# A fused attention and gated-FFN kernel: when its tail asks for its loads and forms its weight sums

## The chip, the cores and the metric

The kernel runs on one core of one Trainium2 chip. The metric is the device time of one execution in microseconds (us); the time before is the median of three runs.

Engines are named as in the profile: PE is TensorE (PEld its weight loads), DVE is VectorE, ACT is ScalarE, POOL is GpSimd, and SP is the engine whose queue issues most DMA transfers here.

## The reference

For `x` of 2048 rows and 512 columns, two branches are computed and mixed with a gate per row:

```python
g = _sigmoid((x * gate_w).sum(-1, keepdims=True))
a = _A_ref(x, A_wqkv, A_wo)              # attention, 32 heads of 16, causal window of 256, then @ wo
b = (_silu(x @ w_gate) * (x @ w_up)) @ w_down     # w_gate, w_up: 512 x 1792, w_down: 1792 x 512
return g * a + (1 - g) * b
```

## The kernel before, in words

Everything is kept transposed: features lie on the 128 partitions, positions along the rows, in four chunks `c` of 512 positions. An f32 product is made of three matmuls (`mm3`, L88 to L90): each operand is split into a rounded high part and a low part, and high x high, high x low and low x high are added up in PSUM. The split of an operand (`split`) costs one ACT instruction for the high part (L70) and one DVE instruction for the low part (L73).

The body computes attention, and beside it the gate and up products of the FFN. Attention's heads go to a DRAM tile `od`, the FFN's activated products to a DRAM tile `kept_h` (14 row tiles `f`, 4 chunks). The **tail** (class `B` in the code, from L685 on) does what is left:

1. `last_tile(c)` for the four chunks: the last FFN tile (L770, 24 matmuls each). Between them the weights `wo` are split (`late`).
2. Sixteen items `("a", c, k)`: the output projection of attention. An item has 12 matmuls. After the fourth item of a chunk four PSUM banks hold its result; DVE multiplies each with the gate (`attn`, L905 or L902) and POOL's queue sends it to `outT`. Even chunks use the banks `ps1` and `ps2`, odd ones `pa` and `pb`, so item 8 writes banks that items 0 to 3 filled.
3. The down projection by a Strassen-Winograd scheme: seven products in the order `ORDER = (1, 5, 6, 3, 7, 2, 4)`, 14 items of 6 matmuls each. The item with index `WO` = 16 is the first of product 1.

The operands of the seven products are made of four quarters of `kept_h`, called `x`, `v`, `y` and `z` (L814), 14 pieces `j` of 256 KB each: product 1 takes x, 5 takes v, 6 takes v + z, 3 takes z, 7 takes (v + z) - x, 2 takes y and 4 takes v + z + y. `combine` (L817) makes the sums on DVE. On the weights' side product 1 takes the left half of `w_down` (`load_left`, L753, then a split), and products 5, 6, 3 and 7 take sums of blocks: `sums(k)` for k = 4, 5, 6 loads two tiles of `w_down` (L185), forms four block sums on DVE (L192, four instructions), splits them (`high` on ACT, L846; `low` on DVE, L850) and stores them in a DRAM tile `sd` (L854), from where `load_sum` (L837) brings them back into the tiles `wh` and `wl`, about 6 items ahead of use.

The order in every queue is the order of the code. The main loop goes over the items `n`; in each round it issues a load of an attention item (`got<-od`, L738), then what the table `DO[n]` holds (filled with `on(n, ...)` and `steps`), then `load_sum`, then the split of item n + LEAD (`halve`, LEAD = 4), then one job (`JOBS`: the evacuation of a PSUM bank), and then the item's matmuls:

```python
for n, e in enumerate(ITEMS[:end]):
    if n + LEAD + AHEAD < WO: load(ITEMS[n + LEAD + AHEAD])
    for f in DO.pop(n, ()): f()
    ...
    if n + LEAD < len(ITEMS): halve(ITEMS[n + LEAD])
    if JOBS: JOBS.pop(0)()
    ...
```

An engine that waits in the middle of its row holds up everything behind it. The split parts `hh` and `hl` have six buffers, so the split of item n + 4 waits until PE has done item n - 2. The tiles `got` have ten buffers, used in turn. A transfer on SP's queue waits for the one issued eight before it on that queue, since the completion flags are eight and used in turn.

Of the kernel before, what the change touches and what calls it, by code (L numbers as in the profile page):

```python
# [12 lines left out]
ALU = mybir.AluOpType  # L13
# [13 lines left out]
LEAD = 4  # L27
# [9 lines left out]
def gated_mix(ctx, tc, xT, xn, wqk, wv, wo, wgu, wd, gw, outT):  # L37
# [30 lines left out]
    def split(hi, lo, src, hi_eng, lo_eng):  # L68
        if hi_eng is nc.scalar:
            nc.scalar.copy(hi, src)  # L70
        else:
            hi_eng.tensor_copy(hi, src)
        lo_eng.tensor_tensor(out=lo, in0=src, in1=hi.bitcast(F32), op=ALU.subtract)  # L73
# [31 lines left out]
    def slot(name, dtype=F32R):  # L105
        return stk.tile([P, S], dtype, name=name)
# [56 lines left out]
    def left(k, m, place):  # L163

        for n in range(m):
            LEFT[k + n] = [place[:, (h * m + n) * HD:(h * m + n + 1) * HD] for h in range(2)]
        return halves_of(place)
# [557 lines left out]
    with ExitStack() as B:  # L725
# [7 lines left out]
        def column():  # L733
            return hp.tile([P, CH], F32, name="sg", bufs=4)

        def taken(src):
            t = got.tile([P, CH], F32, name="got")
            nc.sync.dma_start(t, src)  # L738
            return t

        def load_wo(k):
            raw = taken(wo[:, k])
            return lambda: split(woh[:, k], wol[:, k], raw, nc.scalar, nc.vector)

        def x_slot(n, dtype=F32R):
            return const.tile([P, NK * CH], dtype, name=f"x{('hi', 'lo')[n % 2]}{n // 2}")
# [3 lines left out]
        def load_left(k, m):  # L750

            raw = got.tile([P, CH], F32, name="got")
            nc.sync.dma_start(raw[:, :m * HD].rearrange("p (m c) -> p m c", m=m), wd[k:k + m, :, :HD].rearrange("m p c -> p m c"))  # L753

            def halves():
                n = k // 4
                if ("left", n) not in PLACE:
                    PLACE["left", n] = x_slot(1 - n)
                place = PLACE["left", n][:, k % 4 * D:(k % 4 + m) * D]
                split(*left(k, m, place), raw[:, :m * HD], nc.scalar, nc.vector)  # L760
            return halves

        def last_tile(c):

            f, gu = NF - 1, []
            for i, name in enumerate(("pa", "pb")):
                ps = pp.tile([P, CH], F32, name=name)
                todo = products(("f", f, i), c)
                for n, (w, x) in enumerate(todo):
                    nc.tensor.matmul(ps, w, x, start=n == 0, stop=n == len(todo) - 1)  # L770
                gu.append(ps)
            h = z_place(NP - 1 if c % 2 else NP // 2, c // 2)
            nc.scalar.activation(h, gu[0], AF.Tanh, scale=0.5)
            nc.vector.scalar_tensor_tensor(h, h, 1.0, gu[0], op0=ALU.add, op1=ALU.mult)
            nc.vector.scalar_tensor_tensor(h, h, half_sign(f, c), gu[1], op0=ALU.mult, op1=ALU.mult)
            return lambda: nc.sync.dma_start(kept_h[f, c], h)

        ORDER = (1, 5, 6, 3, 7, 2, 4)
        ITEMS = [("a", c, k) for c in range(NCH) for k in range(NK)]
        WO = len(ITEMS)  # L780
        for p in ORDER:
            ITEMS += [(p, k, pr) for k in range(NP) for pr in range(2)] if p != 4 else [(p, k, pr) for pr in range(2) for k in range(NP)]

# [2 lines left out]
        def by_four(t):  # L786
            return t.rearrange("p (k n) -> p k n", k=NK)
# [21 lines left out]
        def fetch_part(what, k, pr):  # L809

            odd, f, where = {"x": (0, 0, x_place), "v": (1, 0, v_place), "y": (0, NP, z_place), "z": (1, NP, z_place)}[what]
            t = PARTS[what, k, pr] = where(k, pr)
            if what != "z" or k < NP - 1:
                nc.sync.dma_start(t, kept_h[k + f, 2 * pr + odd])  # L814
# [7 lines left out]
        def load(e):  # L822

            _, c, k = e
            heads = od[2 * k:2 * k + 2].rearrange("g (j e) s -> (g j) e s", e=32)
            SRC[e] = taken(heads[:, :DH, c * CH:(c + 1) * CH])
# [61 lines left out]
        def gates(n):  # L888
            GATE[n] = by_four(x_slot(7, F32) if n else slot("k11", F32))
            nc.sync.dma_start(GATE[n].rearrange("p k n -> p (k n)"),  # L890
                              gd[16 * n:16 * n + 16].rearrange("c q i -> (c q i)")[None, :].to_broadcast([P, S]))
# [28 lines left out]
        def bank(p, pr):  # L920
            if p in (1, 6, 7, 4):
                pool, name = ((ps1, "ps1"), (ps2, "ps2"))[pr]
            else:
                pool, name = pp, ("pa", "pb")[pr]
            if name not in BANK or BANK[name][0] != p and p in (5, 2, 3):
                BANK[name] = p, [pool.tile([P, CH], F32, name=name) for _ in range(2)]
            return BANK[name][1]
# [47 lines left out]
                if p == 4 and pr == 0:  # L975
                    JOBS.append(lambda d=d: scaled(2 * pr, 2 + d, column(), two[d]))

        AHEAD = 6
        late = [load_wo(k) for k in range(NK)]
        gates(0)  # L980
        store = last_tile(0)
        for f in late[:2]:
            f()
        late += [load_left(k, m) for k, m in ((0, 2), (2, 2), (4, 2), (6, 1))]
        for e in ITEMS[:2]:
            load(e)
        for j in range(3):
            fetch_part("z", *divmod(j, 2))
        last_tile(1)
        store()  # L990
        for f in late[2:4]:
            f()
        for e in ITEMS[2:LEAD]:
            load(e)
        for j in range(3, 6):
            fetch_part("z", *divmod(j, 2))
        store = last_tile(2)
        for f in late[4:]:
            f()
        for e in ITEMS[LEAD:LEAD + AHEAD]:  # L1000
            load(e)
        for j in range(4):
            fetch_part("x", *divmod(j, 2))
        for e in ITEMS[:3]:
            halve(e)
        last_tile(3)
# [9 lines left out]
        def on(n, f, *args):  # L1016
            DO.setdefault(n, []).append(lambda: f(*args))

        for j in range(2 * NP):
            two = divmod(j, 2)  # L1020
            n = WO + j
            if j > 3:
                on(j + 2, fetch_part, "x", *two)
            on(n, fetch_part, "v", *two)
            if j > 5:
                on(n + 4, fetch_part, "z", *two)
            on(n + 13, combine, "v", "z", ALU.add, *two)
            on(n + 27, combine, "x", "x", ALU.subtract, *two)
            on(n + 40, fetch_part, "y", *two)
            on(n + 48 + 22 * (j > 7), combine, "v", "y", ALU.add, *two)  # L1030
        on(WO + 24, gates, 1)
        on(WO + 12, lambda: PLACE.update({6: by_four(x_slot(6, F32))}))

        def steps(n, first, f, *args):
            todo = []
            on(n, lambda: todo.extend(f(*args)))
            for m, i in enumerate(first):
                on(i, lambda m=m: todo[m]())
        steps(0, range(4, 8), sums, 4)
        steps(6, range(WO, WO + 4), sums, 5)  # L1040
        steps(13, range(WO + 4, WO + 8), sums, 6)
        for i in range(NP):
            n = WO + 57 + 4 * (i // 2) + i % 2 - (i == 6)
            steps(n, (n + 6, n + 7), negated, NP + i)
        for n, e in enumerate(ITEMS[:end]):
            if n + LEAD + AHEAD < WO:
                load(ITEMS[n + LEAD + AHEAD])
            for f in DO.pop(n, ()):
# [10 lines left out]
            p, k, pr = e  # L1059
# [6 lines left out]
        two, t, part, rest = bank(4, 1), *(column() for _ in range(3))  # L1066
# [46 lines left out]
```

## Time and profile before

| | us |
|---|---|
| median of three runs (812.82, 813.27, 810.50) | 812.82 |
| the profiled execution, its own time | 810.65 |
| its span, first to last instruction | 808.9 |
| PE busy in the span | 801.3 |
| DVE busy | 627.2 |
| ACT busy | 432.8 |
| POOL busy | 346.1 |

Times within the profile count from the start of the span. The tail's matmuls begin at 602.1 us (the first one of L770). A row of the timeline gives the start, the duration (of a merged run of instructions: from the first start to the last end), the engine, the line, the operation with what it writes and reads, the count, and in brackets how long the engine stood idle before and what ended that. Matmuls are pipelined: a row's 0.39 us is the passage of one of them, and the distance of two starts is the rate.

### The profile page before, as it was taken

The numbers are of one execution on the slowest core, as the hardware profiler recorded it, in microseconds if no ns is written. First come the engines' busy times: TensorE is split into PE (matmuls) and PEld (weight loads), VectorE is DVE, ScalarE is ACT, GpSimd is POOL, SyncE is SP. The second block draws the span as 40 slices with busy tenths as digits, with TensorE's granted clock in tenths as the row PEclk, the third lists the DMA queues.
The fourth block names the chain that finished last, engine by engine and source line by source line (L and its number), as shares of the span: only waits on it lengthen the run. The fifth ranks groups of instructions, "written<-read, shape, count | busy, mean of one in ns | idle before, by whom it ended". The sixth has DMA issues, their size and how long they took to land.

```text
span 808.9 us, 21548 instructions
## 1 busy us (share of the span) xinstructions
PE 801.3 (99%) x8251; PEld 680.3 (84%) x8251; DVE 627.2 (78%) x1685; ACT 432.8 (54%) x882; POOL 346.1 (43%) x647
## 2 busy tenths in 40 slices
PE   9999999999999999999999999999999999999998
PEld 7888998889888889888887988888878878888886
DVE  5397787878886887888776878797775368998896
ACT  6412656565566567555666656555643324554642
POOL 7712556565546456544656454446630021000212
PEclk9999999999999999999999999999999999999999
DMA  8574415425242353352433526426548797618435
GB/s 297 167 204 157 139 68 141 124 88 150 70 151 82 108 167 111 103 154 69 139 108 116 150 62 181 155 77 205 167 132 284 249 374 266 238 50 274 93 56 101
DMA packets 61963, 121.88 MB, mean 151 GB/s; under 512 B 10852, under 2 KB 19556, under 8 KB 61604
## 3 DMA queue, kind: packets, MB, share of 16 engines
q1 hardware_dynamic: 54756, 99.27, 39.9%
q0 software_dynamic: 7104, 21.24, 8.9%
q8 instruction: 65, 1.06, 0.6%
q14 instruction: 38, 0.31, 0.1%
HBM read 55.97 MB, written 39.34 MB: 118 GB/s over the span
## 4 chain that ended last, share of the span: by engine, by line
PE 91%; DMA 5%; DVE 2%; SPq 1%; issue 0%; ACT 0%; ACTq 0%; DVEq 0%
PE pb L252 24%; PE pa L252 24%; PE pb L365 7%; PE ps L302 6%; PE ps L341 5%; PE ps L88 4%; PE ps L89 4%; PE ps L90 3%; DMA got<-od 2%; PE pb L232 2%; PE pa L232 2%; PE ps L365 2%; PE pb L88 1%; PE pa L88 1%; PE pa L89 1%; PE pb L89 1%
## 5 line engine op out<-in xcount | busy, mean ns | idle before, releaser
L304 DVE CUSTOM_DVE_ANT_0 ps<-ps,mask 128x384 f32<-128x384 f32 (+2 forms) x512 | 268.5, 541 | 102.1 <-PE ps L341 49.0
L343 ACT ACTIVATE pt<-ps 128x384 f32<-128x384 f32 (+2 forms) x512 | 238.2, 475 | 130.5 <-PE ps L302 65.6
L345 POOL TENSOR_SCALAR_AFFINE_SELECT pt<-pt 128x256 f32<-128x256 f32 x256 | 110.2, 431 | 200.0 <-ACT pt L343 199.6
L341 PE MATMUL ps<-q,k 64*128 64x384 f32 (+2 forms) x512 | 161.2, 333 | 0.0
L302 PE MATMUL ps<-k,q 63*128 63x384 f32 (+2 forms) x512 | 159.4, 331 | 0.5 <-DVE mx L304 0.5
L252 PE MATMUL pb<-xhi,wh 64*128 64x512 f32 x512 | 115.5, 395 | 0.1
L252 PE MATMUL pb<-xlo,wh 64*128 64x512 f32 x512 | 114.1, 391 | 0.0
L252 PE MATMUL pb<-xhi,wl 64*128 64x512 f32 x512 | 113.9, 391 | 0.0
L252 PE MATMUL pa<-xhi,wh 64*128 64x512 f32 x512 | 113.3, 393 | 0.0
L252 PE MATMUL pa<-xlo,wh 64*128 64x512 f32 x512 | 112.1, 391 | 0.0
L252 PE MATMUL pa<-xhi,wl 64*128 64x512 f32 x512 | 112.0, 391 | 0.0
L302 PEld LDWEIGHTS ps<-k,q 63*128 63x128 f32 x512 | 88.7, 185 | 17.8 <-issue 5.7
L348 POOL TENSOR_SCALAR_AFFINE_SELECT pt<-pt 128x256 f32<-128x256 f32 x224 | 99.1, 443 | 0.0
L341 PEld LDWEIGHTS ps<-q,k 64*128 64x128 f32 x512 | 90.5, 184 | 5.3 <-issue 0.8
L365 PE MATMUL ps<-pt,vg 64*32 64x320 f32 (+4 forms) x1408 | 75.0, 346 | 0.0
L365 PE MATMUL pb<-pt,vg 64*32 64x320 f32 (+3 forms) x1360 | 73.9, 350 | 0.0
L304 DVE DVE_READ_ACCUMULATOR2_ANT mx<- 128x1 f32 x512 | 71.7, 140 | 0.0
L365 PEld LDWEIGHTS pb<-pt,vg 64*32 64x32 f32 x1360 | 46.4, 106 | 28.2 <-DVE mx L304 5.2
L252 PEld LDWEIGHTS pb<-xhi,wh 64*128 64x128 f32 x512 | 60.8, 185 | 6.2 <-DVE o L382 0.6
L252 PEld LDWEIGHTS pb<-xhi,wl 64*128 64x128 f32 x512 | 60.6, 184 | 5.2
L252 PEld LDWEIGHTS pa<-xhi,wl 64*128 64x128 f32 x512 | 58.9, 184 | 5.6
L252 PEld LDWEIGHTS pa<-xhi,wh 64*128 64x128 f32 x512 | 59.0, 186 | 3.7
(305 smaller groups left out, 1633.8 us busy)
## 6 DMA issues: line engine op xcount, KB each, us to landing
kept_h<-ev SPq DMA_DIRECT2D x52, 256.0 KB
od<-o POOLq DMA_DIRECT2D x32, 256.0 KB, 3.7
raw<-wgu SPq DMA_DIRECT2D x28, 256.0 KB
q<-xhi SPq DMA_DIRECT2D x56, 128.0 KB
k<-xhi SPq DMA_DIRECT2D x56, 128.0 KB
outT<-sg POOLq DMA_DIRECT2D x28, 256.0 KB, 4.2
vd<-vs POOLq DMA_DIRECT2D x8, 672.0 KB, 4.8
vg<-vd SPq DMA_DIRECT2D x32, 168.0 KB
```

What stands on the lines that cost most here:

```text
L88: nc.tensor.matmul(ps, lh, rh, start=start and i == 0, stop=False, skip_group_check=skip)
L89: nc.tensor.matmul(ps, lh, rl, start=False, stop=False, skip_group_check=skip)
L90: nc.tensor.matmul(ps, ll, rh, start=False, stop=stop and i == n - 1, skip_group_check=skip)
L232: nc.tensor.matmul(ps, w, x, start=n == 0, stop=n == len(todo) - 1)
L252: mm = nc.tensor.matmul(ps[me], w[r], x[r], start=not second and i == 0, stop=bool(second) and i == n - 1)
L302: nc.tensor.matmul(ps[:, :n], QT[g % 2][pr][r, q0:q0 + P], KT[g % 2][pr][r, k0:k0 + n], start=True, stop=True)
L304: mx = nc.vector.tensor_tensor_reduce(out=ps[:, :n], in0=ps[:, :n], in1=mask[:, 3 * P - n:], scale=1.0, scalar=NEG, op0=ALU.add, op1=ALU.m ...
L341: nc.tensor.matmul(ps[:, :n], KT[g % 2][pr][r, k0:k0 + P], QT[g % 2][pr][r, k0:k0 + n], start=True, stop=True)
L343: BEHIND.append(nc.scalar.activation(pt[:, j, :n], ps[:, :n], AF.Exp, scale=SCALE))
L345: nc.gpsimd.affine_select(out=pt[:, :, :P], in_=pt[:, :, :P], pattern=[[0, 2], [1, P]], compare_op=ALU.is_ge, fill=0.0, base=0, channel_mu ...
L348: nc.gpsimd.affine_select(out=pt[:, :, 2 * P:], in_=pt[:, :, 2 * P:], pattern=[[0, 2], [-1, P]], compare_op=ALU.is_ge, fill=0.0, base=-1, ...
L365: nc.tensor.matmul(AV[g, c][h][32 * j:32 * j + 32, q0 - c * CH:q1 - c * CH], VG[4 * g + kb // 4][o, kb % 4, 17 * j:17 * j + 32], PT[g, kb, ...
```

## The change

The tail's begin and the table `DO` are rewritten; no computation is added or taken away.

- Begin: the loads of the first four items stand right behind those of `wo` and ahead of the gate's broadcast (`gates(0)`, L890). The four `load_left`, the first six `z` and the first four `x` leave the begin.
- `x` piece j is asked for at item j + 2 for all j; `z` piece j at item WO + j + 9 (before: the first six at the begin, the others at WO + j + 4).
- The four `load_left` stand at items 6, 8, 10 and 12, their splits at items 10, 12, 14 and 16.
- `sums(4)`: load at item 1 (before 0), block sums, high, low and store at items 9 to 12 (before 4 to 7). `sums(5)` and `sums(6)` keep their places.
- `combine` v + z at WO + j + 18 (before + 13), v - x at WO + j + 32, and 4 later for the last four j (before + 27), v + y at WO + j + 50, and 22 later for j of 6 and more (before + 48, and 22 later for j of 8 and more).
- The second broadcast of the gate at WO + 34 (before + 24).

```diff
-        WO = len(ITEMS)
+        WO, AHEAD = len(ITEMS), 6
...
-        AHEAD = 6
         late = [load_wo(k) for k in range(NK)]
+        for e in ITEMS[:LEAD]:
+            load(e)
         gates(0)
         store = last_tile(0)
         for f in late[:2]:
             f()
-        late += [load_left(k, m) for k, m in ((0, 2), (2, 2), (4, 2), (6, 1))]
-        for e in ITEMS[:2]:
+        for e in ITEMS[LEAD:AHEAD]:
             load(e)
-        for j in range(3):
-            fetch_part("z", *divmod(j, 2))
         last_tile(1)
         store()
-        for f in late[2:4]:
+        for f in late[2:]:
             f()
-        for e in ITEMS[2:LEAD]:
+        for e in ITEMS[AHEAD:AHEAD + LEAD]:
             load(e)
-        for j in range(3, 6):
-            fetch_part("z", *divmod(j, 2))
         store = last_tile(2)
-        for f in late[4:]:
-            f()
-        for e in ITEMS[LEAD:LEAD + AHEAD]:
-            load(e)
-        for j in range(4):
-            fetch_part("x", *divmod(j, 2))
         for e in ITEMS[:3]:
             halve(e)
...
-            if j > 3:
-                on(j + 2, fetch_part, "x", *two)
+            on(j + 2, fetch_part, "x", *two)
             on(n, fetch_part, "v", *two)
-            if j > 5:
-                on(n + 4, fetch_part, "z", *two)
-            on(n + 13, combine, "v", "z", ALU.add, *two)
-            on(n + 27, combine, "x", "x", ALU.subtract, *two)
+            on(n + 9, fetch_part, "z", *two)
+            on(n + 18, combine, "v", "z", ALU.add, *two)
+            on(n + 32 + 4 * (j > 9), combine, "x", "x", ALU.subtract, *two)
             on(n + 40, fetch_part, "y", *two)
-            on(n + 48 + 22 * (j > 7), combine, "v", "y", ALU.add, *two)
-        on(WO + 24, gates, 1)
+            on(n + 50 + 22 * (j > 5), combine, "v", "y", ALU.add, *two)
+        on(WO + 34, gates, 1)
...
-        steps(0, range(4, 8), sums, 4)
+        for n, (k, m) in enumerate(((0, 2), (2, 2), (4, 2), (6, 1))):
+            on(6 + 2 * n, lambda n=n, k=k, m=m: on(10 + 2 * n, load_left(k, m)))
+        steps(1, range(9, 13), sums, 4)
```

What this does to the rows of SP's queue, from the loads of `wo` at the tail's begin: before they stand as follows (`od` are attention's heads, `kept_h` into `q` the z pieces, into `xhi` the x pieces, `wd` into `got` the left half, `gd` the gate, `kept_h<-q` a store of the last tile).

```order
L738 DMA got<-wo 128x512 x4
L890 DMA k_10631<-gd 128x2048
L753 DMA got<-wd 128x2x256 x3
L753 DMA got<-wd 128x256
L738 DMA got<-od 128x1x512 x2
L814 DMA q_10679<-kept_h 128x512 x3
L776 DMA kept_h<-q_10659 128x512
L738 DMA got<-od 128x1x512 x2
L814 DMA q_10679<-kept_h 128x512
L814 DMA q_10659<-kept_h 128x512 x2
L738 DMA got<-od 128x1x512 x6
L814 DMA xhi_10776<-kept_h 128x512 x4
```

After the change the same place reads as follows; `wd` into `xlo` is the load of `sums(4)`.

```order
L738 DMA got<-wo 128x512 x4
L738 DMA got<-od 128x1x512 x4
L890 DMA k_10639<-gd 128x2048
L738 DMA got<-od 128x1x512 x2
L776 DMA kept_h<-q_10667 128x512
L738 DMA got<-od 128x1x512 x4
L776 DMA kept_h<-q_10667 128x512
L738 DMA got<-od 128x1x512 x2
L185 DMA xlo_10821<-wd 128x512 x2
L738 DMA got<-od 128x1x512
L814 DMA xhi_10842<-kept_h 128x512
L738 DMA got<-od 128x1x512
```

Twelve of the attention loads now stand ahead of the load of `sums(4)` with nothing but the gate and two stores between them; the z pieces are gone from here, and the x pieces and the left half come behind.

On DVE, around the first block sums (L192), before: these rows begin with the splits of items 3 to 7; the L905 rows evacuate the banks of items 0 to 3.

```order
L73 TENSOR_TENSOR hl<-got,hh 128x512 x5
L192 TENSOR_TENSOR xlo_10829<-xlo_10829 128x256 x4
L73 TENSOR_TENSOR hl<-got,hh 128x512
L905 TENSOR_TENSOR sg<-ps_10836,k_10631 128x512
L73 TENSOR_TENSOR hl<-got,hh 128x512
L905 TENSOR_TENSOR sg<-ps_10837,k_10631 128x512
L850 TENSOR_TENSOR xlo_10829<-xlo_10829 128x512 x2
L73 TENSOR_TENSOR hl<-got,hh 128x512
L905 TENSOR_TENSOR sg<-ps_10838,k_10631 128x512
```

After the change the four evacuations of items 0 to 3 (`ps_`) and the first of items 4 to 7 (`pa`) are ahead of it; `xlo_11029` is the split of the left half.

```order
L905 TENSOR_TENSOR sg<-ps_10806,k_10639 128x512
L73 TENSOR_TENSOR hl<-got,hh 128x512
L905 TENSOR_TENSOR sg<-pa,k_10639 128x512
L192 TENSOR_TENSOR xlo_10821<-xlo_10821 128x256 x4
L73 TENSOR_TENSOR hl<-got,hh 128x512
L905 TENSOR_TENSOR sg<-pa,k_10639 128x512
L73 TENSOR_TENSOR xlo_11029<-got,xlo_11029 128x512
L73 TENSOR_TENSOR hl<-got,hh 128x512
L905 TENSOR_TENSOR sg<-pb,k_10639 128x512
L850 TENSOR_TENSOR xlo_10821<-xlo_10821 128x512 x2
L73 TENSOR_TENSOR hl<-got,hh 128x512
L905 TENSOR_TENSOR sg<-pb,k_10639 128x512
```

The third place is SP's queue late in product 1, where the first block sums come back from `sd` for product 5. Before, 12 loads of v and z stand between the last store into `sd` and these rows.

```order
L814 DMA k_11356<-kept_h 128x512 x2
L837 DMA wl<-sd 128x512
L837 DMA wh<-sd 128x512
L837 DMA wl<-sd 128x512
L890 DMA xlo_11511<-gd 128x2048
L837 DMA wh<-sd 128x512
```

After the change 14 such loads stand between the last store into `sd` and the first `wl` row, and four more behind it.

```order
L814 DMA q_10667<-kept_h 128x512 x3
L837 DMA wl<-sd 128x512
L814 DMA k_11420<-kept_h 128x512 x2
L837 DMA wh<-sd 128x512
L814 DMA k_11420<-kept_h 128x512 x2
L837 DMA wl<-sd 128x512
```

The broadcast of the gate (L890) has gone from this stretch to a later one, and z pieces stand between the loads of the sums.

## The prediction

> **What bounds the kernel now.** I read the page's first part, then PE's waits in the tail, then the tail cut into stretches, and then the timelines of PE, DVE and SP around the one stretch that stands out.
>
> ```profile
> span 808.9 us, 21548 instructions
> PE 801.3 (99%) x8251; PEld 680.3 (84%) x8251; DVE 627.2 (78%) x1685; ACT 432.8 (54%) x882; POOL 346.1 (43%) x647
> PE ps L88 <- DVE sg L905: 1.6, 2, 1.4
> 623.87:645.75 21.88, 21.88 (x98) 1.00 0.75 242
> 645.75:653.18 7.43, 5.81 (x18) 0.77 0.97 344
> 653.18:671.34 18.16, 18.16 (x82) 1.00 0.85 320
> 671.34:690.38 19.04, 19.04 (x86) 1.00 0.92 319
> 690.38:802.58 112.20, 112.20 (x497) 1.00 0.52 132
> ```
>
> PE is the bound: 801.3 of 808.9 us. The change adds no PE work, so it can only fill a hole or make one. The third line is all that PE waits for in the tail: twice for an evacuation (L905). The windows (length, PE busy with its count, granted clock, DMA share, GB/s) place it: only 645.75 to 653.18 has idle PE, and there the granted clock is 0.77. The last two stretches give the full rate: product 1 is 84 matmuls in 19.04 us, 226.7 ns each, and 690.38 to 802.58 is 495 matmuls (the rest of the 14 item products, the last one cut short), which at that rate take 112.2 us. After product 1 begins nothing is lost.
>
> What the hole costs, from PE's rows of items 8 and 9 (start, duration; in brackets the idle time before):
>
> ```profile
> 645.75 0.39 PE L88 MATMUL ps<-hh,woh 128*128 128x512 f32 x1
> 646.21 0.39 PE L90 MATMUL ps<-hh,wol 128*128 128x512 f32 x1
> 646.77 0.50 PE L88 MATMUL ps<-hh,woh 128*128 128x512 f32 x1 [0.18 <-DVE sg L905]
> 647.34 0.40 PE L90 MATMUL ps<-hh,wol 128*128 128x512 f32 x1
> 649.18 0.69 PE L88 MATMUL ps<-hh,woh 128*128 128x512 f32 x1 [1.44 <-DVE sg L905]
> 652.95 0.39 PE L88 MATMUL ps<-hh,woh 128*128 128x512 f32 x1
> ...
> 671.34 0.39 PE L88 MATMUL ps<-hh,xlo 128*128 128x512 f32 x1
> ```
>
> Item 8 begins at 645.75 and product 1 at 671.34, 25.59 us for eight items of 12 matmuls; at 226.7 ns these take 21.76. **The hole costs 3.83 us.** Its parts: 646.21 to 646.77 is 0.33 over one step, 646.77 to 647.34 0.12, 647.34 to 649.18 1.61, and the nine matmuls from 649.18 to 652.95 take 3.77 us instead of 2.04, so 1.73 is lost to the slower clock after the pause.
>
> Why the evacuation was late, in DVE's rows and SP's:
>
> ```profile
> 633.81 0.69 DVE L73 TENSOR_TENSOR hl<-got,hh 128x512 fp32r<-128x512 f32 x1 [0.78 <-ACT hh L70]
> 642.36 1.80 DVE L192 TENSOR_TENSOR xlo<-xlo 128x256 f32<-128x256 f32 x4 [7.85 <-DMA xlo<-wd]
> 644.68 0.68 DVE L905 TENSOR_TENSOR sg<-ps,k 128x512 f32<-128x512 f32 x1
> 646.64 1.28 DVE L850 TENSOR_TENSOR xlo<-xlo 128x512 fp32r<-128x512 f32 x2
> 648.44 0.68 DVE L905 TENSOR_TENSOR sg<-ps,k 128x512 f32<-128x512 f32 x1
> 634.37 1.53 SPq L185 DMA_DIRECT2D xlo<-wd  x2
> ```
>
> DVE stands still for 7.85 us before the first block sums, because their two tiles of w_down were asked for only at 634.37 to 635.90 and landed at 642.36. The evacuations of items 0 to 3 stand behind in DVE's row, although their banks were full when item 3 ended, four items or 10.9 us before item 8. The two that PE waited for start at 646.03 and 648.44, between leftovers such as L850. This stop is the one thing to remove.
>
> **The change, part by part.**
>
> *First block sums.* Counting back from 645.75, items 0 to 7 (96 matmuls) begin at about 623.98, when the last tile's matmuls end and its buffers come free. The load for the sums now stands at item 1, behind twelve attention loads, of which the last waits only for splits that are ready by then; I place it at 624.5. The same pair of transfers took up to 8 us in the old queue, so it lands by 632.5. Its use moves from item 4 to item 9. There the sums stand behind the evacuation of item 7's first bank, complete at 645.75: margin about 13 us. The evacuations of items 0 to 3 are now ahead of the sums, and need only their banks (full at 623.98 + 10.88 = 634.86) and one split each; the last follows the split of item 11, which waits for PE to end item 5 at 640.3, and is done near 642.3, while item 8 asks for that bank at 645.75 + 2.04 = 647.8. No pause there: **-3.83 us**.
>
> *What fills items 8 to 11 on DVE instead.* The row then holds four evacuations (0.68 each), three splits of items (0.69), the block sums (1.80), low (1.28) and the first split of the left half (0.69 at most, below): 645.75 + 2.72 + 2.07 + 1.80 + 1.28 + 0.69 = 654.3 if nothing waits. Item 12 needs the banks from 645.75 + 4 x 2.72 = 656.6, the last one from 658.7. So 4.4 us are left: 0. If this cover were gone (one more landing wait of 4.4 us on DVE), the old pause would return at item 12.
>
> *Left half.* Four ACT and four DVE splits go from the begin to items 10 to 16:
>
> ```profile
> 619.36 1.29 DVE L73 TENSOR_TENSOR xlo<-got,xlo 128x512 fp32r<-128x512 f32 x2
> 620.56 1.02 DVE L73 TENSOR_TENSOR xhi<-got,xhi 128x512 fp32r<-128x512 f32 x2
> 681.93 1.29 DVE L73 TENSOR_TENSOR hl<-xhi,hh 128x512 fp32r<-128x512 f32 x2
> ...
> 684.94 0.39 PE L88 MATMUL ps<-hh,xhi 128*128 128x512 f32 x1
> ```
>
> The first two rows are 2.3 us of DVE that delay nothing at either place, since in the attention items an item lasts 2.72 us. Only the last, 0.42 us, falls into product 1, where item 26 is the tightest split: done at 682.6 (third row, a merged run of two), used by the second matmul after 684.94, 2.5 us later. That margin falls to 2.1: 0.
>
> *x, z, and the sums' way back.* x pieces are asked for ten items ahead of their split, all behind light traffic: 0. For z and the sums in `sd` the queue of late product 1 counts:
>
> ```profile
> 682.46 1.25 SPq L814 DMA_DIRECT2D got<-kept_h  x2
> 690.15 0.32 SPq L837 DMA_DIRECT2D wl<-sd  x1
> 701.26 0.39 PE L88 MATMUL pa<-hh,wl 128*128 128x512 f32 x1
> DMA to landing us min/median/max: 5.2/5.6/6.4
> ```
>
> Twelve transfers from 682.46 put the first `wl` at 690.15, 0.64 us each, 11.1 us before its matmul. Now 14 stand ahead: 8.97 us. Its matmul comes 3.83 earlier, at 697.4. If the start of this burst moves with PE (the store ahead of it waits for DVE's low), `wl` is issued at 687.6, 9.8 us early; if the start stays at 682.46, at 691.4, 6.0 us early. The nearest landing time that the trace gives under a full queue is that of the stores to `outT`, 5.2 to 6.4 us (last row). Ends: 0 and a pause of 0.4 us. I take 0, since the begin of the burst hangs on DVE, which follows PE. The z sums have more: z piece 0 is the second transfer of the burst and is combined only at item WO + 18, 9 items or 12.2 us after the item that asks for it.
>
> *Later combines and gate.* 42 combines of 0.69 us before and after. Two more of the v + y ones fall on items WO + 84 and 85 beside evacuations of product 2:
>
> ```profile
> 783.05 0.69 DVE L817 TENSOR_TENSOR xlo<-xlo,k 128x512 f32<-128x512 f32 x1
> 783.72 0.69 DVE L73 TENSOR_TENSOR hl<-got,hh 128x512 fp32r<-128x512 f32 x1
> ```
>
> DVE works there without a gap until 783.72 (starts 0.60 to 0.67 apart), two operations to an item of 1.36 us. Two more make it 1.2 us late; the splits run four items, 5.4 us, ahead. 0 either way; the row would have to be 4 us later to hold PE. The second gate broadcast moves out of the full queue and is used 20 items later at the earliest: 0.
>
> **Sum.** -3.83 us, and +0 to +0.4. Against the profiled execution (810.65): 806.8. That execution lies 2.17 below the median of the runs, 812.82; by a constant offset the median becomes 809.0. But the stall hangs on a landing time, and is the only wait of the tail, so a part of the runs' spread (810.50 to 813.27) may be the stall itself. I take 808.0, between 806.8 and 809.0.
>
>
> **Rivals.**
>
> 1. *A pause remains* (a landing or DVE's fuller row at items 8 to 12 holds one bank). For it: L905 is still one of up to seven operations around the sums. Against: 4.4 us of margin. A pause as long as the 1.61, without the slow clock, leaves -2.2: 810.0 beside the forecast; with the slow clock 3.3 are lost and only 0.5 gained, 811.3.
> 2. *The change doesn't do it.* The evacuations may be held by the tiles that they write:
>
> ```profile
> 652.34 0.69 DVE L905 TENSOR_TENSOR sg<-pa,k 128x512 f32<-128x512 f32 x1 [1.42 <-DMA outT<-sg]
> ```
>
> Here one waits 1.42 us for a store to land. If that were the cause, the hole stays: 812.8. Against it: this is after PE's pauses, when evacuations came 1.2 us apart; at one per item of 2.72 us the fourth buffer back is 10.9 us old, more than any landing of 6.4.
> 3. *Slower: the third block sums inherit the stop.*
>
> ```profile
> 657.93 0.81 SPq L185 DMA_DIRECT2D xlo<-wd  x2
> 677.05 1.79 DVE L192 TENSOR_TENSOR xlo<-xlo 128x256 f32<-128x256 f32 x4
> ```
>
> Their load overwrites the tile that the first sums are stored from, so it waits for that store, which moves from item 7 to item 12, to about 653. Use moves from 677.05 to 673.2. If the load keeps its old distance from the store (9.6 us after 648.3) it starts at 662.6, and with 8 us of landing it is there at 670.6, 2.6 early. DVE would stop if it landed after 673.2, and with the 2.1 us of margin PE would pause after 675.3. Every us beyond costs one, and 1.73 more for the clock; the kernel is slower by over 0.3% from a landing at 680 on, say 816. It needs twice the longest landing seen.
>
> 4. *The slow clock has another cause and stays.* Then only the pauses go, 0.33 + 0.12 + 1.61 = 2.1 us, and the time is 1.7 above the forecast, 809.7. Against it: in the windows above the clock is under 1.00 in this one stretch, and the slow matmuls begin with the one that ends the longest pause. [...]
>
> **How the numbers follow.** 0.3% (2.4 us) is about what a measurement of this kernel can tell from no change, so the bounds are 810.4 and 815.3. Forecast 67%, own range 806.3 to 809.5; a remaining pause 17%; no effect 6%; the third sums 6%; the clock 4%. Faster: 0.9 of the forecast (the rest for the spread of runs), 0.3 of rival 1 and half of rival 4, 0.67. Slower: rival 3, 0.06. The same: what is left, 0.27. The range reaches from 805.8 (the profiled execution's 806.8 less 1.0 for runs whose stall was longer) to 811.3, the far end of rival 1.
>
> **What would show it.** Right: the window around item 8 has PE busy throughout at clock 1.00; no wait of PE on L905; the first L192 of the tail starts near 646.4 without an idle time put down to `wd`; product 1 begins near 667.5 and product 5 at 19.04 later. Wrong: a wait of PE at item 12 (rival 1), a clock under 1.00 anywhere in the tail, L905 waiting for `outT` (rival 2), the L192 of the third sums idle for `wd` (rival 3), or a wait on `wl` at the begin of product 5's second half.

## The result, and the profile after

| | us |
|---|---|
| kernel after, median of 6 runs (805.57 to 808.00) | 807.28 |
| kernel before, median of 6 runs beside them (810.21 to 814.63) | 812.08 |
| ratio, 95% interval | 0.9937 (0.9915 to 0.9959) |
| profiled execution after, its time and its span | 805.57, 803.9 |

From the page of the kernel after, the span and the engines, and then the windows over its tail (length, PE busy and count, PE's weight loads, DVE, ACT, POOL, granted clock, DMA share, GB/s), cut at the first matmul of the tail, of item 8, of product 1 and of product 5:

```profile
span 803.9 us, 21546 instructions
PE 798.0 (99%) x8251; PEld 679.7 (85%) x8251; DVE 626.9 (78%) x1685; ACT 432.4 (54%) x882; POOL 346.0 (43%) x647
600.87:644.53 43.66, 43.66 (x198) 36.15 (x193) 22.60 (x37) 13.19 (x23) 4.30 (x7) 1.00 0.77 250
644.53:666.29 21.76, 21.76 (x98) 18.02 (x96) 16.26 (x29) 8.93 (x16) 2.96 (x6) 1.00 0.95 341
666.29:685.33 19.04, 19.04 (x86) 15.77 (x84) 14.69 (x25) 10.60 (x18) 2.16 (x4) 1.00 0.91 311
685.33:797.53 112.20, 112.20 (x497) 92.91 (x495) 102.09 (x161) 56.02 (x92) 11.91 (x14) 1.00 0.57 147
```

PE is busy in the whole of the tail at clock 1.00, and the list of PE's waits has no row from 600 us on. Items 8 to 15 take 21.76 us, what 96 matmuls take at 226.7 ns. From the tail's first matmul to product 1 it is 65.42 us; before it was 671.34 - 602.10 = 69.24. **The difference, 3.82 us, is the hole.** The rest of the 5.0 us between the two spans lies ahead of the tail, which began 1.23 us earlier in this execution, in code that the change doesn't touch.

DVE's and SP's timelines of the kernel after, around the first block sums and at the places named in the prediction:

```profile
640.55 0.69 DVE L905 TENSOR_TENSOR sg<-ps,k 128x512 f32<-128x512 f32 x1
643.27 0.68 DVE L905 TENSOR_TENSOR sg<-pa,k 128x512 f32<-128x512 f32 x1
643.87 1.79 DVE L192 TENSOR_TENSOR xlo<-xlo 128x256 f32<-128x256 f32 x4
651.48 0.68 DVE L905 TENSOR_TENSOR sg<-pb,k 128x512 f32<-128x512 f32 x1
672.01 1.79 DVE L192 TENSOR_TENSOR xlo<-xlo 128x256 f32<-128x256 f32 x4
...
622.73 1.08 SPq L185 DMA_DIRECT2D xlo<-wd  x2
658.36 0.82 SPq L185 DMA_DIRECT2D xlo<-wd  x2
686.68 0.32 SPq L837 DMA_DIRECT2D wl<-sd  x1
```

None of these DVE rows has a bracket: DVE comes to the sums and their tiles are there. The four evacuations of items 0 to 3 are done by 641.24, 3.3 us ahead of item 8. The load of the first sums is issued at 622.73 instead of 634.37. The third sums' load (658.36) and their start (672.01) show no stop either.

### The profile page after: what moved, and what is told of

Same layout as the page of the kernel before. It is cut to its first block, busy times and chain, and to the rows that moved or that the text cites. A ratio compares the mean times of both kernels' runs of the same rounds, so it can differ in the third digit from the quotient of the medians.

```text
span 803.9 us, 21546 instructions
## 1 busy us (share of the span) xinstructions
PE 798.0 (99%) x8251; PEld 679.7 (85%) x8251; DVE 626.9 (78%) x1685; ACT 432.4 (54%) x882; POOL 346.0 (43%) x647
## 4 chain that ended last, share of the span: by engine, by line
PE 98%; DVE 2%; issue 0%; POOL 0%; POOLq 0%
PE pa L252 24%; PE pb L252 24%; PE pb L365 7%; PE ps L302 6%; PE ps L341 5%; PE ps L88 4%; PE ps L89 4%; PE ps L90 4%; PE pa L232 2%; PE pb L232 2%; PE ps L365 2%; PE pb L88 2%; PE pa L88 2%; PE pa L89 2%; PE pb L89 2%; PE pb L90 2%
```

## The experiments

Each run has the kernel before timed beside it on the same chip; ratios are to that one. "Hole" is the time from the tail's first matmul to product 1, less the 65.42 us that it takes undisturbed; "B" is the start of the first block sums on DVE. All are read from one profiled execution of each kernel.

### Each half of the change alone

The kernel before with only the block sums moved (e1_sums_only):

```diff
-        steps(0, range(4, 8), sums, 4)
+        steps(0, range(9, 13), sums, 4)
```

> The kernel before with one edit: the first block sums, their split and their store at items 9 to 12 instead of 4 to 7; their load and all other loads stay. My theory (DVE stood in front of the evacuations of items 0 to 3, waiting for the sums' tiles): the tiles land near 642 as before, the sums stand behind the evacuations now, PE has no wait in the tail, the window around item 8 is at clock 1.00, 3.8 us below the kernel before, ratio about 0.994 to 0.995. Rival (the queue of loads at the tail's begin is the cause, late attention tiles with it): the pause stays at least in part, gain under 2 us. Rival (evacuations wait for their stores to outT): no gain.

Measured: 807.19 us (806.00 to 810.16), ratio 0.9937 (0.9915 to 0.9960). The profile has no wait of PE in the tail and no hole; the load is at 634.16 as before, B at 647.38 with no stop.

The kernel after with the sums put back (e2_loads_only):

```diff
-        steps(1, range(9, 13), sums, 4)
+        steps(0, range(4, 8), sums, 4)
```

> The kernel after with one edit back: load of the first block sums at item 0 and the sums at items 4 to 7, as before, while the loads at the tail's begin are the changed ones. My theory: the load is issued near 622.5 (PE's end of the last tile frees its place) instead of 634.4 and lands near 630, about when DVE comes to it (after the split of item 7 near 629.7), so DVE stops for 1 us at most instead of 7.85, no wait of PE, as fast as the kernel after, ratio about 0.994. Rival (the place of the sums in DVE's row is what matters, not the load): DVE's row is held long enough that PE waits for L905 at item 8 again, at least 1.5 us slower than the kernel after.

Measured: 806.73 us (806.40 to 807.26), ratio 0.9928 (0.9913 to 0.9943), no hole. From its timelines of SP and DVE:

```profile
623.59 0.81 SPq L185 DMA_DIRECT2D xlo<-wd  x2
...
632.51 1.80 DVE L192 TENSOR_TENSOR xlo<-xlo 128x256 f32<-128x256 f32 x4 [1.91 <-DMA xlo<-wd]
```

The load is 11 us earlier than in the kernel before, and DVE stops for 1.91 us (1 at most was expected) instead of 7.85, far ahead of item 8. Either half removes the hole in these profiles.

The kernel after with the combines, the second gate broadcast and z's requests at their old distances (e3_old_combines):

```diff
-            on(n + 9, fetch_part, "z", *two)
-            on(n + 18, combine, "v", "z", ALU.add, *two)
-            on(n + 32 + 4 * (j > 9), combine, "x", "x", ALU.subtract, *two)
+            on(n + 4, fetch_part, "z", *two)
+            on(n + 13, combine, "v", "z", ALU.add, *two)
+            on(n + 27, combine, "x", "x", ALU.subtract, *two)
...
-            on(n + 50 + 22 * (j > 5), combine, "v", "y", ALU.add, *two)
-        on(WO + 34, gates, 1)
+            on(n + 48 + 22 * (j > 7), combine, "v", "y", ALU.add, *two)
+        on(WO + 24, gates, 1)
```

> The kernel after, with the places of the combines (v + z, v - x, v + y) and of the second gate broadcast as before, and z asked for at WO + j + 4 for all j. My theory: these places are worth nothing, as fast as the kernel after (within 0.2%), no wait of PE in the tail; DVE may stop for a z piece before a combine. Rival (the later combines are needed once z is asked for late): DVE waits for z at item WO + 13, splits come late, PE waits in product 5, over 1 us slower than the kernel after.

Measured: 806.41 us (806.34 to 806.54), ratio 0.9923 (0.9906 to 0.9940), no hole. The kernel after once more (e5_after_again), unchanged:

> The kernel after, unchanged, for a second profile and for times on the same chip as the others. My theory: 0.994 of the kernel before, no wait of PE in the tail, product 1 begins 65.4 us after the tail's first matmul as in the first profile (before: 69.2), while the body's length moves by about 1 us between executions. Rival (the body's 1.2 us are part of the change): the tail's begin comes at 600.9 again, near 602.1 only in profiles of the kernel before.

Measured: 806.24 us (805.89 to 806.71), ratio 0.9922 (0.9906 to 0.9937), no hole; 666.61 - 601.19 is 65.42 again. So the later combines are worth nothing that these runs can tell. The tail begins at 601.19 here, between 601.31 and 601.72 in the other three, and between 601.21 and 602.10 in the three profiles of the kernel before: the body moves by itself.

### How large the hole is

The kernel before, unchanged, twice more (e0_before_again, e0_before_third).

> The kernel before, unchanged, for a second profile. My theory (the hole hangs on a landing time and on the clock, and is most of the spread of the runs of before): the hole between the first matmul of item 8 and that of product 1 is there again, but of another size than 3.83 us, with another stop of DVE before the block sums; the body's length agrees with the other profiles within about 1 us. Rival (the hole is the same in every execution, the spread comes from the body): 3.83 us within 0.2, and the body differs.

> The kernel before once more, for a third profile; the expectations are those of the second.

Measured: 813.63 and 813.31 us, one execution each. PE's waits in the tail of e0_before_again, then its rows of SP, DVE, ACT and PE around item 8, and in the second block DVE's and PE's of e0_before_third:

```profile
PE ps L88 <- ACT hh L70: 2.2, 1, 2.2
PE ps L88 <- DVE sg L905: 2.0, 3, 1.4
...
637.15 1.53 SPq L185 DMA_DIRECT2D xlo<-wd  x2
644.85 1.80 DVE L192 TENSOR_TENSOR xlo<-xlo 128x256 f32<-128x256 f32 x4 [7.56 <-DMA xlo<-wd]
647.17 0.68 DVE L905 TENSOR_TENSOR sg<-ps,k 128x512 f32<-128x512 f32 x1
637.18 0.62 ACT L70 CAST hh<-got 128x512 fp32r<-128x512 f32 x1 [0.62 <-DMA got<-od]
646.23 1.14 ACT L846 CAST xlo<-xlo 128x512 fp32r<-128x512 f32 x2 [8.42 <-DVE xlo L192]
647.27 2.17 ACT L70 CAST hh<-got 128x512 fp32r<-128x512 f32 x4
648.00 0.47 PE L88 MATMUL ps<-hh,woh 128*128 128x512 f32 x1 [2.20 <-ACT hh L70]
651.67 0.50 PE L88 MATMUL ps<-hh,woh 128*128 128x512 f32 x1 [1.44 <-DVE sg L905]
674.36 0.39 PE L88 MATMUL ps<-hh,xlo 128*128 128x512 f32 x1
```

```profile
644.33 1.80 DVE L192 TENSOR_TENSOR xlo<-xlo 128x256 f32<-128x256 f32 x4 [7.72 <-DMA xlo<-wd]
647.48 0.47 PE L88 MATMUL ps<-hh,woh 128*128 128x512 f32 x1 [2.45 <-ACT hh L70]
651.15 0.79 PE L88 MATMUL ps<-hh,woh 128*128 128x512 f32 x1 [1.23 <-DVE sg L905]
674.03 0.39 PE L88 MATMUL ps<-hh,xlo 128*128 128x512 f32 x1
```

DVE stops about as long as in the first profile, but two to three us later, since SP gets to the load later (637.15 instead of 634.37). The hole is 6.96 and 7.40 us. A further wait has come, ahead of item 8's first matmul. The profile puts it down to ACT's `hh`. But item 8's split is issued in item 4 and `high` in item 5, so item 8's `hh` is the row at 637.18, and the one that ends near 647.9 is item 9's. What ends beside it is the first evacuation, at 647.17 + 0.68 = 647.85, which frees the bank that this matmul writes; so by the order of the code the first bank is late too. In these two profiles the first matmul of item 8 starts at B + 3.15. In all three the seventh, the first that writes the third bank, starts at B + 6.82: 651.67 - 644.85, 651.15 - 644.33, and 649.18 - 642.36 in the first profile, where B + 3.15 is 645.51, just ahead of item 8. The rest follows from when B comes.

### Making the stop on purpose

The kernel after with the load of the sums one item ahead of use (e4_late_load), or in the same item (e6_later_load):

```diff
-        steps(1, range(9, 13), sums, 4)
+        steps(8, range(9, 13), sums, 4)       (e4_late_load)
+        steps(9, range(9, 13), sums, 4)       (e6_later_load)
```

> The kernel after, with the first block sums' load at item 8, one item ahead of their use instead of eight; the uses stay at items 9 to 12. My theory (what costs is DVE stopping in front of evacuations until the tiles land): the load is issued near 645, lands 6 to 8 us later, DVE stops from about 644 to 651 to 653, and the evacuations of items 4 to 7 come late for item 12: PE pauses there by 0.5 to 2 us, and if the pause is long enough the clock falls for about 3.5 us (1.7 us more); 0.5 to 4 us slower than the kernel after. Rival (evacuations have slack enough even so, the place of the sums alone matters): no wait of PE, as fast as the kernel after.

> As the one before, with the load in the same item as its use (item 9). My theory: issued one item later, so the stop of DVE is up to 2.7 us longer, PE pauses by about 2 to 3 us at item 12, and the nine or so matmuls behind a pause of over 1.4 us are 0.43 us apart; 3 to 5 us slower than the kernel after, more than with the load at item 8. Rival on the clock (it has another cause than the pause): the pause comes without a clock under 1.00, and the loss is the pause alone.

Measured: e4_late_load 807.30 us, ratio 0.9942 (0.9919 to 0.9966); e6_later_load 806.87, ratio 0.9946 (0.9927 to 0.9966). (Two of the nine executions of e4_late_load took 1313 and 1592 us, which nothing here explains; the ratio leaves them out, and the median of the other seven is 806.92.) No hole in either. Rows of DVE and PE of e4_late_load:

```profile
650.27 1.80 DVE L192 TENSOR_TENSOR xlo<-xlo 128x256 f32<-128x256 f32 x4 [5.00 <-DMA xlo<-wd]
...
656.96 0.68 DVE L905 TENSOR_TENSOR sg<-pb,k 128x512 f32<-128x512 f32 x1
667.60 0.39 PE L88 MATMUL ps<-hh,xlo 128*128 128x512 f32 x1
```

Both expectations were wrong here: a stop of 5.00 us at this place costs nothing. Item 12 begins at 667.60 - 10.88 = 656.7 and asks for its fourth bank at 658.8; the last evacuation ends at 657.64, 1.1 us before. The later load of e6_later_load was in fact issued no later (641.14 against 642.01), and DVE stopped for 4.94 us, so the pair tells nothing about a longer stop. No pause of PE came in either, so what both expectations say of the clock behind one was not shown here; it was the author's estimate from the first profile of the kernel before (1.73 us lost behind the pause of 1.44 us, at a granted clock of 0.50 from 649.50 to 652.60).

So the stop was made where it had been. In the kernel after the sums go back to items 4 to 7, and all x pieces (e7_x_ahead), or these and four z pieces (e8_x_z_ahead), are asked for ahead of their load:

```diff
-            on(j + 2, fetch_part, "x", *two)
+            on(0, fetch_part, "x", *two)
-            on(n + 9, fetch_part, "z", *two)
+            on(n + 9 if j > 3 else 0, fetch_part, "z", *two)     (e8_x_z_ahead alone)
...
-        steps(1, range(9, 13), sums, 4)
+        steps(0, range(4, 8), sums, 4)
```

> The kernel after with the first block sums back at items 4 to 7 (load at item 0), and all 14 x pieces asked for at item 0, ahead of that load. My theory, from the three profiles of the kernel before: if the sums start on DVE at time B, PE can start the seventh matmul of item 8 (the third bank, freed by the third evacuation) at B + 6.8 us and not earlier, so the pause is (B + 6.8) less the undisturbed start, item 8 + 1.36; none while B is at least 5.5 us ahead of item 8. The 14 transfers of about 0.7 us put the load near 631 and B near 638 to 641 with item 8 at 644.5 to 645.5: a stop of DVE of 7 us or more, a pause of PE between 0 and 2 us, time 806 to 810. Rival (any such stop of DVE costs PE the same 4 us or more): 810 or more.

> As the one before, with four z pieces more ahead of the load of the sums. My theory: B is 2 to 4 us later, near 641 to 645, the seventh matmul of item 8 at B + 6.8, a pause of 1 to 5 us and 1.7 to 2.6 us more for a slow clock behind it, time 810 to 814, as the kernel before. Rival on the clock (another cause): a pause without slow matmuls behind it.

Measured: e7_x_ahead 808.70 us (807.88 to 810.67), ratio 0.9970 (0.9947 to 0.9993); e8_x_z_ahead 813.98 (810.44 to 815.93), ratio 1.0023 (0.9997 to 1.0048). DVE's and PE's rows, first of e7_x_ahead, then of e8_x_z_ahead:

```profile
641.67 1.81 DVE L192 TENSOR_TENSOR xlo<-xlo 128x256 f32<-128x256 f32 x4 [10.72 <-DMA xlo<-wd]
648.50 0.50 PE L88 MATMUL ps<-hh,woh 128*128 128x512 f32 x1 [1.25 <-DVE sg L905]
669.55 0.39 PE L88 MATMUL ps<-hh,xlo 128*128 128x512 f32 x1
```

```profile
644.84 1.80 DVE L192 TENSOR_TENSOR xlo<-xlo 128x256 f32<-128x256 f32 x4 [14.17 <-DMA xlo<-wd]
648.00 0.47 PE L88 MATMUL ps<-hh,woh 128*128 128x512 f32 x1 [2.39 <-ACT hh L70]
651.66 0.79 PE L88 MATMUL ps<-hh,woh 128*128 128x512 f32 x1 [1.02 <-DVE sg L905]
674.43 0.39 PE L88 MATMUL ps<-hh,xlo 128*128 128x512 f32 x1
```

The seventh matmul is at B + 6.83 and B + 6.82, as written down ahead. A stop of 10.72 us that ends early makes a hole of 2.07; one of 14.17 that ends 3.2 us later makes 7.22 and brings the time of the kernel before back. What counts is when the stop ends, not how long it is. Counted from the tail's first matmul, B comes at 39.61 us in e7_x_ahead, 40.26 in the first profile of the kernel before, 42.87 in e0_before_again, 43.05 in e8_x_z_ahead and 43.12 in e0_before_third. The holes rise in this order (2.07, 3.82, 6.96, 7.22, 7.40), the stops do not (10.72, 7.85, 7.56, 14.17, 7.72). Both edits also put five attention loads behind the x pieces; but from B to 657 us DVE has no idle time before a split of an attention tile in either profile, so late tiles did not make these holes.

### The loads' own share

The runs of the sums-only kernel spread to 810.16, so it was profiled again (e1_sums_again).

> The kernel before with only the block sums' items changed, once more, for a second profile, since its runs spread from 806.0 to 810.2 while those with the new loads stay within 1 us. My theory: the splits of attention items still hang on tiles asked for late, so in some executions PE waits for a split (hh or hl) somewhere in items 8 to 15; if this profile is a slow one, it shows such a wait and no wait for L905. Rival: the spread is in the body, ahead of the tail.

Measured: 809.60 us, one execution, with a hole of 3.20. ACT's, DVE's and PE's rows:

```profile
643.41 0.62 ACT L70 CAST hh<-got 128x512 fp32r<-128x512 f32 x1 [4.45 <-DMA got<-od]
648.43 0.62 ACT L70 CAST hh<-got 128x512 fp32r<-128x512 f32 x1 [4.40 <-DMA got<-od]
649.08 0.69 DVE L73 TENSOR_TENSOR hl<-got,hh 128x512 fp32r<-128x512 f32 x1 [3.72 <-ACT hh L70]
649.69 0.68 DVE L905 TENSOR_TENSOR sg<-ps,k 128x512 f32<-128x512 f32 x1
650.43 0.50 PE L88 MATMUL ps<-hh,woh 128*128 128x512 f32 x1 [2.91 <-DVE sg L905]
```

PE does wait for L905, against the letter of the expectation, but not because of the sums: two attention tiles land late under the old queue of loads, ACT waits for them, DVE for ACT, and the evacuation stands behind the split in DVE's row. So the sums' place alone is not safe. By their place in SP's row these tiles and those of the sums are late for the same reason, the queue of loads ahead of them; in the kernel after, ACT's waits in the tail have none for an attention tile, and in e5_after_again, and in e2_loads_only, which has the new loads with the sums at their old place, the longest that DVE stands idle for ACT's `hh` between 618 and 690 us is 2.03 us (3.72 here).

### All profiles together

| profiled execution | time | hole | time less hole |
|---|---|---|---|
| before | 810.65 | 3.82 | 806.8 |
| e0_before_again | 813.63 | 6.96 | 806.7 |
| e0_before_third | 813.31 | 7.40 | 805.9 |
| e8_x_z_ahead | 813.71 | 7.22 | 806.5 |
| e1_sums_again | 809.60 | 3.20 | 806.4 |
| e7_x_ahead | 808.82 | 2.07 | 806.8 |
| after, e5_after_again, e1_sums_only, e2, e3 | 805.57 to 806.40 | 0 | 805.6 to 806.4 |
| e4_late_load, e6_later_load | 806.89, 806.87 | 0 | 806.9 |

Less the hole, all are within 1.3 us, the amount by which the tail's begin moves (600.87 to 602.18).

## Why the prediction was right, and what was off

It named 808.0 in a range of 805.8 to 811.3, and 0.67 for faster; measured were 807.28, and 806.24 in the second set of runs.

- **The cause held.** DVE stood in front of the evacuations waiting for the tiles of the first sums; with the load early, or the sums later, PE's wait for it is gone (e2, e1_sums_only), and putting the wait back brings the old time back (e8). The first e1 profile alone would have said that the sums' place is enough; the second shows a hole of 3.20 from late attention tiles.
- **The term of the hole was sized from the smallest of three profiled cases.** The prediction's -3.83 is what this pair of profiles shows (3.82). But the other two profiles of the kernel before have holes of 7.0 and 7.4. Its runs beside the later experiments go from 807.53 to 816.62; against the 805.6 to 806.9 that the profiles leave without the hole, that would be holes of about 1 to 10 us, an estimate, since those runs have no profile. The median of the runs fell by 4.8 in the first comparison (812.08 to 807.28) and by 6.4 in the second (812.60 to 806.24). The step that guarded against it was the choice of 808.0 below the constant-offset 809.0, since the stall might be a part of the runs' spread; in the three profiles the hole moves by 3.6 us and the rest by 0.9, so it is most of it. The drop forecast, 812.82 - 808.0 = 4.8, equals the first one measured partly by luck: in the second it was 6.4.
- **What fills items 8 to 11.** The margin was put at 4.4 us, counted from item 7's first bank at 645.75. This step took that bank to be full only when item 7 ends; its last matmul is the third of the item's twelve, and the evacuation came at 643.27, 1.3 us ahead of item 8. So the first L192 came at 643.87 and not near 646.4 (1.2 us of this are the body's). In e4 1.1 us were left after a stop of 5.00, so the margin was about 6.1 us there, and the one more landing wait of 4.4 us, with which the prediction saw the pause return, would not have been enough.
- **Left half, x, z, combines, gate at 0.** Held: no wait of PE in any of them, and e3 ties with the kernel after. The first `wl` was issued at 686.68, 9.5 us ahead of its matmul at 685.33 + 8 x 1.36 = 696.2; the prediction had 9.8 to 6.0.
- **Rival 1, a pause that remains,** did not come in a profile of the kernel after. Its 810.0 is not its own sum, 808.0 + 1.61 = 809.6.
- **Rival 2, the tiles that evacuations write:** did not hold the bank; the waits on `outT` come behind the hole, and DVE's waits in the tail of the kernel after show none.
- **Rival 3, the third sums:** their load was issued at 658.36 and they started at 672.01, without a stop. Its figure is off too: a landing at 680, 4.7 us behind 675.3, gives 808.0 + 4.7 + 1.73 = 814.4, still below 815.3, where slower begins. Neither slip bears on the forecast.
- **Rival 4, the clock.** The term of 1.73 was the clock's share in one execution, not a fixed part of a pause. In e7_x_ahead (1.25 and 0.23 us idle) and in e1_sums_again (2.91 us) no matmul behind the pause is 0.43 us apart; the kernel before had such matmuls after 0.18 and 1.44. The slow clock was seen only with a hole: in the profiles without one no two matmuls that follow each other in PE's rows from 610 to 690 us start more than 0.23 us apart.

## What to carry to other kernels

Where an engine works in order and one of its steps waits for a transfer, count what stands behind that step and when PE needs it: here not the length of the stop, but the time at which it ended set the loss (a stop of 10.72 us cost 2.07, one of 7.72 us cost 7.40). Requests for late use, put at the begin of a stage, cost something here by delaying the requests behind them (the load of the first sums was issued at 634.37 us behind them, at 622.73 without them); order a queue of loads by time of use. And take a second profile of the kernel before when its runs spread by an amount near the gain that is sought (here 2.8 us over three runs, for a hole of 3.8), since one profile may show a small case.

## What the runs showed of the hardware

In these profiles the clock after a pause does not follow from the length of that pause alone. From PE's waits in the tail of e1_sums_again and its window over the pause, and the window of e0_before_third from item 8 on:

```profile
PE ps L88 <- DVE sg L905: 2.9, 1, 2.9
647.00:654.00 7.00, 4.09 (x19) 3.06 (x18) 4.70 (x9) 2.78 (x5) 1.08 (x2) 1.00 0.92 279
...
644.64:656.01 11.37, 7.36 (x19) 4.69 (x18) 9.63 (x18) 4.56 (x8) 2.70 (x5) 0.71 1.04 313
```

A pause of 2.91 us left the granted clock at 1.00 (window 647.00 to 654.00), while pauses of 0.18 and 1.44 us in the kernel before were followed by nine matmuls at about half the rate (0.43 us apart instead of 0.227; the granted clock was 0.50 from 649.50 to 652.60), and the window of e0_before_third, whose pauses were 2.45 and 1.23 us, has a clock of 0.71. The two pauses of the kernel before add up to 1.62 us, less than the one that left the clock at 1.00. What else decides is not shown by these runs.
